# A sparse attention and two expert layers on one core: products with v in two chunks, and copies and sums in another order

## The chip, the core and the metric

The kernel runs on one core of a Trainium2 chip, in one launch. The metric is the device time in microseconds, of which each kernel has several runs; the median counts. Besides the times there is one execution that the hardware profiler recorded. The engines are TensorE (PE in the profile), VectorE (DVE), ScalarE (ACT), GpSimd (POOL) and SyncE (SP), which issues transfers.

## What is computed

An attention over 4 batches of 8 heads, 576 tokens of width 64, in which only scores within tau of a row's greatest are kept; then a layer with eight experts, of which each token uses the one with the greatest gate; then a layer with four experts whose outputs are all summed by given weights. Tokens are 2304, of width 512.

```python
scores = scale * np.matmul(q, k.transpose(0, 1, 3, 2))
thresh = np.max(scores, axis=-1, keepdims=True) - tau
scores = np.where(scores >= thresh, scores, -1000000000.0)
scores = scores - np.max(scores, axis=-1, keepdims=True)
attn = np.exp(scores)
attn = attn / (np.sum(attn, axis=-1, keepdims=True) + 1e-09)
x = np.matmul(attn, v)                      # then 2304 tokens of width 512
...
# first layer: one expert of eight for each token
expert_idx = np.argmax(x @ w_gate, axis=1)  # gate_w: its softmax probability
out[mask] = gate_w[mask, None] * (np.maximum(x[mask] @ w1[e], 0.0) @ w2[e])
...
# second layer: all four experts for each token
out += p[:, e:e + 1] * (np.maximum(x @ w1[e], 0.0) @ w2[e])
```

Sizes: w1 and w2 of the first layer are 8 x 512 x 1024 and 8 x 1024 x 512, of the second 4 x 512 x 1024 and 4 x 1024 x 512, all float32.

## The kernel before

Matmuls run on float32 numbers that are split in two parts: a high part, rounded by a cast ("H"), and a low part, the difference ("low"). A product is then three matmuls (H by H, H by low, low by H). So each operand costs a cast, mostly on ScalarE, and a subtraction, on VectorE or GpSimd.

**Attention** (lines 1040 to 1114) is one loop over 144 steps t: 16 pairs of heads, nine blocks of queries each. A step writes its instructions in a fixed order: the exponential of the block before (`expp`, L751, ScalarE), the scores of the next block (`mm_s`, L733 and L734, TensorE, two banks `s`), the row maximum of its own (`maxx`, L742, VectorE, and `nm`, L745, GpSimd), the mask of two blocks ago (`mask`, L762, VectorE), what waits in the queue `dq` (copies of finished products, L833, VectorE), transpositions of the next pair's q and k (L583), the transpositions of four blocks ago (`transp`, L781 to L799) with their copies `PT` on ScalarE (L785 to L800), one item of the queue `xq`, and items of the products with v. Transpositions and products share four PSUM banks `t`.

The products of a pair are two halves of the queries. Each has five items: `first`, a matmul with the last 64 keys of both heads in one 128 x 128 tile `vl` (L816), and four of two matmuls with 64-column tiles `vt` (L822); a copy `ev` to `outT` follows each half. A matmul is two records in the trace, and two in the rows below that read x2. A pair's items become ready at t = 9p + 13. They go out at steps with t % 3 == 1, as evenly over the chunks left as they divide. In the steady loop these chunks are 4, 3 and 3 items, so that the first half ends within the second chunk. Pair 13 has five chunks. After pair 15 begins (t > 135) another rule spreads them. The queue `xq` holds for each batch the gate's logits, its routing (`route`, L110 to L190: VectorE, ScalarE and GpSimd, with the scatter transfers of rows) and, later, the first expert work; one item goes out in each step.

**First expert layer** (363 to 578 us): 72 weight units, cast and lowered in `split` (L360) as they arrive, by `dosplit`, whose rule gives each unit's low part to VectorE or GpSimd.

**Second layer** (from 589 us): three phases of 768 tokens with 16 steps each (`l1` and `l2`). A step's first product is Strassen-like: seven products of blocks (L1356 to L1358, tile `w`) of the weights' blocks with the tokens' blocks `yc0` to `yc6`, and sums of these on VectorE (`q`, `r`, `c`, L1365; relu on ScalarE, L1370, its low on VectorE, L1371). The first product's result is copied by ScalarE (`p1`, L1375) before VectorE may add to it; then `l1` calls its argument `mid`. The tokens' blocks need four sums (`sums`, L1326: t[1], b12, t[0], t[2]), and each block a cast (L1222) and a low (L1181). `first_blocks` (L1433) writes this for the first step and is its `mid`. Weights come by `prep1(j)` (POOL sums `sx`, ScalarE casts `hl`, GpSimd lows; it casts what it can and returns the cast of `sx` for `mid`) and `prep2(j)` (ScalarE cast `v2hl`, L1212, GpSimd low). The loop at L1445 writes, for step j, `prep1(j + 2)`, `prep2(j + 1)` and the next transfer on SyncE's queue, `l2(j)`, then the `l1` that takes `mid`. Steps 0, 16 and 32 begin a phase.

Of the kernel before, what the change touches and what calls it, by code (L numbers as in the profile page):

```python
# [11 lines left out]
F32 = mybir.dt.float32  # L12
# [3 lines left out]
AF = mybir.ActivationFunctionType  # L16
# [16 lines left out]
def kernel(  # L33
# [99 lines left out]
    def route(t0, nt, pspool, xtile):  # L133
# [35 lines left out]
        for j in range(nt):  # L169
            free_scatter("xs", xs, desti[:, t0 + j : t0 + j + 1], xtile(j))  # L170
        nc.vector.tensor_copy(dest[:, t0 : t0 + nt], desti[:, t0 : t0 + nt])
        yield "scatter"

        ex = small([128, 5, 8], "ex")[:, :nt]
        nc.scalar.activation(ex, d, AF.Exp)
        sg = small([128, 5], "sg")[:, :nt]
# [257 lines left out]
    def dosplit(i, eH=None, eL=None):  # L434
        if i < len(units):
            hls[i] = split(raws.pop(i), eH or "a", eL or ("v" if i % 8 < 3 or i in (3, 4) else "g"), i)

# [18 lines left out]
    def attention(actx):  # L456
# [10 lines left out]

        PG = 3
        NWARM = (36, 3, 3, 3)
# [569 lines left out]
        t = 0  # L1039
        while t < NTT + LT + LP:  # L1040
# [57 lines left out]
            for _ in range(min(len(xq), 1 if t < NTT + LM else 3)):  # L1098
                if xq[0] in frees or not fq and not busy and (xq[0] is not early_start or t >= 9 * last):
                    xq.popleft()()  # L1100
            if pv and (t % PG == 1 or t > 9 * last):
                d = pv[0][2]
                n = max(1, (d + DX - t) // (1 if t > 9 * last else PG))
                n = -(-sum(x[2] == d and x[0].__name__ != "ev" for x in pv) // n)
                while pv and (n or pv[0][0].__name__ == "ev"):
# [210 lines left out]
    with tc.tile_pool(name="m2", bufs=1) as mp, tc.manual_schedule():  # L1316
# [9 lines left out]
        def sums(ph, e):  # L1326
# [3 lines left out]
            for o, a, b_ in ((t[1], b22, b12), (b12, b12, b11), (t[0], b22, b12), (t[2], b21, t[0])):  # L1330
                sub(nc.gpsimd if o is t[2] else e, o, a, b_)
                yield
# [9 lines left out]

        def l1(j, mid, first=False):
            if j >= 3 * NS:
# [39 lines left out]
            prod(Z, 5)  # L1384
            r = add("r", Z, q)
            if not first:
                prod(X, 1, True)
                c11 = relu(0, 0, X)
# [44 lines left out]
        def first_blocks():  # L1433
            for _ in range(3):
                next(ahead)
            for _ in parts2(0, (4, 5, 3)):
                pass
            prep2(0)
            next(ahead)
            for _ in parts2(0, (2,)):  # L1440
                pass

        l1(0, first_blocks, True)
        prep1(1)()
        for j in range(3 * NS):  # L1445
            ph, i = divmod(j, NS)
            if j:
                mid = prep1(j + 2)
            prep2(j + 1)
            fetch2(j + 2 if j == 0 else j + 3)  # L1450
# [48 lines left out]
```

## Time and profile before

| what | value |
|---|---|
| median of 3 runs | 1360.22 us (1359.86 to 1360.77) |
| the profiled execution | 1361.25 us |
| its span in the trace | 1358.8 us |
| TensorE busy | 1323.6 us (97%) |
| GpSimd, VectorE, ScalarE busy | 890.4, 865.9, 653.8 us |
| mean granted clock | 0.993 |

The span runs from the first to the last instruction of the trace; 2.45 us of the profiled execution lie around it. An engine is an in-order queue: an instruction that waits holds what is written behind it. A row of the waits gives the engine and its instruction, what it waited for, and the total, the count and the longest. In a timeline a row is a run of like instructions, with the start of the first, from its start to the last one's end, and what ended the idle time before. TensorE's matmuls overlap, so that the ends of its rows are modelled.

### The profile page before, as it was taken

What the parts mean: (1) busy time and instruction counts of PE and PEld (TensorE: products, weight loads), DVE (VectorE), ACT (ScalarE), POOL (GpSimd) and SP (SyncE); (2) the same over time, 40 slices, a digit from 0 to 9 for tenths busy, and PEclk for the clock granted to TensorE, in tenths of its full rate; (3) what the DMA queues carried; (4) which work ended last, traced back from release to release, by engine and by line L of the source; (5) the groups of instructions that cost most, each with busy time, mean ns of one, the idle gap of its engine ahead of it and who ended that gap; (6) DMA issues with size and microseconds to landing.
All of it is one profiled execution on the core that took longest, in us unless ns stands there. A gap on an engine that the chain in (4) does not pass through costs nothing.

```text
span 1358.8 us, 22300 instructions
## 1 busy us (share of the span) xinstructions
PE 1323.6 (97%) x8120; PEld 1169.4 (86%) x8120; DVE 865.9 (64%) x1705; ACT 653.8 (48%) x1239; POOL 890.4 (66%) x945
## 2 busy tenths in 40 slices
PE   8999999999999999979999999999999999999997
PEld 7777777776899999968999998898999989999986
DVE  8878778777843333545566667666666676655664
ACT  7887786866454455633333334333333343333331
POOL 8876766845385444658666766777677657666642
PEclk8999999999999999989999999999999999999999
DMA  5551111103584556522221112222112222222201
GB/s 153 167 158 57 58 55 62 37 17 110 165 239 148 167 177 203 172 64 78 76 80 62 63 62 67 84 99 78 63 62 76 80 68 80 78 70 78 78 16 47
DMA packets 131696, 127.52 MB, mean 94 GB/s; under 512 B 17920, under 2 KB 110080, under 8 KB 131584
## 3 DMA queue, kind: packets, MB, share of 16 engines
q1 hardware_dynamic: 128128, 116.55, 27.4%
q0 software_dynamic: 3456, 9.51, 1.8%
q8 instruction: 66, 1.08, 0.3%
q14 instruction: 46, 0.38, 0.1%
HBM read 107.61 MB, written 18.42 MB: 93 GB/s over the span
## 4 chain that ended last, share of the span: by engine, by line
PE 68%; issue 3%; POOL 2%; ACT 1%; DVE 1%; POOLq 0%; ACTq 0%; DVEq 0%
PE w L366 14%; PE w L367 14%; PE w L368 14%; PE w L1356 8%; PE w L1358 8%; PE w L1357 8%; PE w L395 1%; PE t L822 0%; DVE g L1371 0%; DVE P L762 0%; POOL out_dram L192 0%; DVE c L1365 0%; POOL hl L360 0%; POOL v2hl L1181 0%; ACT v2hl L1212 0%
## 5 line engine op out<-in xcount | busy, mean ns | idle before, releaser
L1356 PE MATMUL w<-yc,hl 128*128 128x384 f32 x672 | 227.3, 338 | 13.5 <-DVE r L1365 6.5
L1181 POOL TENSOR_TENSOR v2hl<-raw,v2hl 128x1024 fp32r<-128x1024 f32 x48 | 116.0, 2416 | 172.2 <-ACT v2hl L1212 172.2
L1357 PE MATMUL w<-yc,hl 128*128 128x384 f32 x672 | 226.5, 337 | 0.5 <-DVE yc L1181 0.5
L1358 PE MATMUL w<-yc,hl 128*128 128x384 f32 x672 | 226.7, 337 | 0.0
L368 PE MATMUL w<-v2hl,g 128*128 128x512 f32 x576 | 225.3, 391 | 0.0
L366 PE MATMUL w<-v2hl,g 128*128 128x512 f32 x576 | 225.2, 391 | 0.0
L367 PE MATMUL w<-v2hl,g 128*128 128x512 f32 x576 | 224.9, 390 | 0.0
L1420 DVE SCALAR_TENSOR_TENSOR y<-w,big,y 128x512 f32<-128x512 f32 x252 | 179.3, 745 | 51.0 <-PE w L368 50.9
L1370 ACT ACTIVATE g<-c 128x384 fp32r<-128x384 f32 x144 | 75.9, 527 | 191.9 <-DVE c L1365 191.9
L360 POOL TENSOR_TENSOR hl<-raw,hl 128x1024 fp32r<-128x1024 f32 x44 | 107.6, 2446 | 90.6 <-ACT hl L356 55.5
L1371 DVE SCALAR_TENSOR_TENSOR g<-c,g 128x384 fp32r<-128x384 f32 x144 | 111.6, 775 | 62.5 <-ACT g L1370 56.3
L745 POOL TENSOR_SCALAR nm<-nm,sc 128x1 f32<-128x1 f32 x144 | 92.6, 643 | 81.9 <-DVE sb L742 56.0
L1356 PEld LDWEIGHTS w<-yc,hl 128*128 128x128 f32 x672 | 127.0, 189 | 17.3 <-ACT p L1375 7.1
L1212 ACT CAST v2hl<-raw 128x1024 fp32r<-128x1024 f32 x48 | 50.5, 1053 | 188.6 <-PE w L368 188.6
L762 DVE SCALAR_TENSOR_TENSOR P<-sb,nm,E 128x576 f32<-128x576 f32 x144 | 133.5, 928 | 9.1 <-issue 3.0
L1357 PEld LDWEIGHTS w<-yc,hl 128*128 128x128 f32 x672 | 127.1, 189 | 2.6 <-DVE yc L1181 0.8
L368 PEld LDWEIGHTS w<-v2hl,g 128*128 128x128 f32 x576 | 108.3, 188 | 23.6 <-DVE g L1371 0.5
L366 PEld LDWEIGHTS w<-v2hl,g 128*128 128x128 f32 x576 | 108.5, 188 | 21.7 <-ACT g L1370 0.6
L1358 PEld LDWEIGHTS w<-yc,hl 128*128 128x128 f32 x672 | 126.9, 189 | 0.0
L367 PEld LDWEIGHTS w<-v2hl,g 128*128 128x128 f32 x576 | 108.4, 188 | 21.4
L1181 POOL TENSOR_TENSOR hl<-sx,hl 128x1024 fp32r<-128x1024 f32 x48 | 115.6, 2409 | 13.8 <-ACT hl L1196 13.8
L1181 POOL TENSOR_TENSOR hl<-raw,hl 128x512 fp32r<-128x512 f32 x96 | 97.2, 1034 | 41.7 <-ACT hl L1196 41.7
(292 smaller groups left out, 3151.4 us busy)
## 6 DMA issues: line engine op xcount, KB each, us to landing
raw<-in_moe_w_dram SPq DMA_DIRECT2D x168, 512.0 KB
xs<-zrow SPq DMA_DIRECT2D x32, 256.0 KB
xrow<-xs SPq DMA_DIRECT2D x18, 256.0 KB
kt<-in_k_dram SPq DMA_DIRECT2D x16, 256.0 KB
qt<-in_q_dram SPq DMA_DIRECT2D x16, 256.0 KB
vt<-in_v_dram SPq DMA_DIRECT2D x16, 256.0 KB
kt<-in_k_dram SPq DMA_DIRECT2D x16, 32.0 KB
qt<-in_q_dram SPq DMA_DIRECT2D x16, 32.0 KB
```

The source lines that it names most:

```text
L360: e.tensor_tensor(hl[:, 1, :], raw, hl[:, 0, :].bitcast(F32), op=ALU.subtract)
L366: nc.tensor.matmul(o, lhsT=aH, rhs=bH, start=first, stop=False)
L367: nc.tensor.matmul(o, lhsT=aH, rhs=bL, start=False, stop=False)
L368: nc.tensor.matmul(o, lhsT=aL, rhs=bH, start=False, stop=last)
L745: g.tensor_scalar(nm[:, 1:2], nm[:, 0:1], sc[:, 2:3], None, op0=ALU.add)
L762: nc.vector.scalar_tensor_tensor(P, sb, nm[:, 1:2], e, op0=ALU.is_le, op1=ALU.mult, accum_out=a)
L1181: e.tensor_tensor(o, a, b_, op=ALU.subtract)
L1356: nc.tensor.matmul(o, lhsT=aH, rhs=bH, start=first, stop=False, skip_group_check=True)
L1357: nc.tensor.matmul(o, lhsT=aH, rhs=bL, start=False, stop=False, skip_group_check=True)
L1358: nc.tensor.matmul(o, lhsT=aL, rhs=bH, start=False, stop=last, skip_group_check=True)
L1371: return lambda: nc.vector.scalar_tensor_tensor(o[1], src, 0.0, o[0].bitcast(F32), op0=ALU.max, op1=ALU.subtract)
L1420: nc.vector.scalar_tensor_tensor(d, w3(o), s_, d, op0=ALU.mult, op1=ALU.add)
```

## The change

Six edits. `route` writes the gate's exponential before a `yield` and not behind it, one step of the loop sooner. `dosplit` gives the last five units' low parts to VectorE. In the loop the products go out at t % 9 in (0, 5), five items each, with the rule for t > 135 as it was. `sums` gives all four sums to the engine e (VectorE in phase 0, GpSimd in 1 and 2; in the latter it was GpSimd before). `first_blocks` writes the fourth sum behind the first part, the cast of `yc2` ahead of `prep2(0)`, and `last_block`, its low, behind `r`. In the loop, at steps 1, 16 and 32, `prep1` and `prep2` are called in `mid`, thus behind the copy `p1`.

```diff
--- before.py
+++ after.py
@@ -169,10 +169,10 @@
         for j in range(nt):
             free_scatter("xs", xs, desti[:, t0 + j : t0 + j + 1], xtile(j))
         nc.vector.tensor_copy(dest[:, t0 : t0 + nt], desti[:, t0 : t0 + nt])
-        yield "scatter"
-
         ex = small([128, 5, 8], "ex")[:, :nt]
         nc.scalar.activation(ex, d, AF.Exp)
+        yield "scatter"
+
         sg = small([128, 5], "sg")[:, :nt]
         nc.vector.tensor_reduce(sg, ex, axis=AX.X, op=ALU.add)
         yield
@@ -433,7 +433,7 @@
 
     def dosplit(i, eH=None, eL=None):
         if i < len(units):
-            hls[i] = split(raws.pop(i), eH or "a", eL or ("v" if i % 8 < 3 or i in (3, 4) else "g"), i)
+            hls[i] = split(raws.pop(i), eH or "a", eL or ("v" if i % 8 < 3 or i in (3, 4) or i >= len(units) - 5 else "g"), i)
 
     def value(ap, engines, top):
         return nc.values_load(ap, engines=engines, min_val=0, max_val=top, skip_runtime_bounds_check_because=no_need)
@@ -465,7 +465,6 @@
         LE, LM, LT, LP = 1, 2, 4, 1
         DX = 1
 
-        PG = 3
         NWARM = (36, 3, 3, 3)
         ET0 = 140
         g = nc.gpsimd
@@ -1098,10 +1097,9 @@
             for _ in range(min(len(xq), 1 if t < NTT + LM else 3)):
                 if xq[0] in frees or not fq and not busy and (xq[0] is not early_start or t >= 9 * last):
                     xq.popleft()()
-            if pv and (t % PG == 1 or t > 9 * last):
+            if pv and (t % 9 in (0, 5) or t > 9 * last):
                 d = pv[0][2]
-                n = max(1, (d + DX - t) // (1 if t > 9 * last else PG))
-                n = -(-sum(x[2] == d and x[0].__name__ != "ev" for x in pv) // n)
+                n = 5 if t <= 9 * last else -(-sum(x[2] == d and x[0].__name__ != "ev" for x in pv) // max(1, d + DX - t))
                 while pv and (n or pv[0][0].__name__ == "ev"):
                     n -= pv[0][0].__name__ != "ev"
                     f, fin, _ = pv.popleft()
@@ -1328,7 +1326,7 @@
             b11, b12, b21, b22 = blocks(ph)
             t = tb[ph] = [mp.tile([128, 2, HT], F32, tag=f"t{x}", name=f"t{x}") for x in range(3)]
             for o, a, b_ in ((t[1], b22, b12), (b12, b12, b11), (t[0], b22, b12), (t[2], b21, t[0])):
-                sub(nc.gpsimd if o is t[2] else e, o, a, b_)
+                sub(e, o, a, b_)
                 yield
 
         def parts2(ph, ms):
@@ -1340,7 +1338,7 @@
                 in_parts(m, src[m])
                 yield
 
-        def l1(j, mid, first=False):
+        def l1(j, mid, first=None):
             if j >= 3 * NS:
                 return mid()
             h = hs[j] = [mp.tile([128, 2, PT], F32R, tag=f"g{x}", name=f"g{j}_{x}", bufs=2) for x in range(2)]
@@ -1383,6 +1381,8 @@
             q = add("q", Y, p1)
             prod(Z, 5)
             r = add("r", Z, q)
+            if first:
+                first()
             if not first:
                 prod(X, 1, True)
                 c11 = relu(0, 0, X)
@@ -1433,20 +1433,26 @@
         def first_blocks():
             for _ in range(3):
                 next(ahead)
-            for _ in parts2(0, (4, 5, 3)):
-                pass
+            for n, _ in enumerate(parts2(0, (4, 5, 3))):
+                if n == 0:
+                    next(ahead)
+            nc.scalar.copy(yc[2][:, 0], tb[0][2])
             prep2(0)
-            next(ahead)
-            for _ in parts2(0, (2,)):
-                pass
-
-        l1(0, first_blocks, True)
+
+        def last_block():
+            sub(nc.vector, yc[2][:, 1], tb[0][2], yc[2][:, 0].bitcast(F32))
+
+        l1(0, first_blocks, last_block)
         prep1(1)()
         for j in range(3 * NS):
             ph, i = divmod(j, NS)
-            if j:
-                mid = prep1(j + 2)
-            prep2(j + 1)
+
+            if j == 1 or j and i == 0:
+                mid = lambda j=j: (prep1(j + 2)(), prep2(j + 1))
+            else:
+                if j:
+                    mid = prep1(j + 2)
+                prep2(j + 1)
             fetch2(j + 2 if j == 0 else j + 3)
             if j == 0:
                 l2(j)
```

TensorE, in the third pair's steps; `P` are the attention's blocks, `PT` their transposed copies, `t` the banks. Before, at the second of the three chunks of the second pair (`PT_698`), one item of its first half, then `first` and one item of the other:

```order
L781 MATMUL t<-ident,P_1064 128x128 x4
L788 MATMUL t<-ident,P_1028 128x128
L789 MATMUL t<-ident,P_1064 64x128
L822 MATMUL t<-PT_698,vt_457 64x288 x2
L816 MATMUL t<-PT_698,vl_116 128x288
L822 MATMUL t<-PT_698,vt_457 64x288 x2
L733 MATMUL s_1152<-kT_865,qHT_119 128x288
```

After, at the second of its two chunks, two steps later in the loop:

```order
L780 MATMUL t<-ident,P_1131 128x128 x4
L787 MATMUL t<-ident,P_1097 128x128
L788 MATMUL t<-ident,P_1131 64x128
L815 MATMUL t<-PT_698,vl_116 128x288
L821 MATMUL t<-PT_698,vt_457 64x288 x8
L732 MATMUL s_1215<-kT_861,qHT_119 128x288
L733 MATMUL s_1215<-kT_861,qLm_123 128x288
```

Behind the transpositions stand now all five items of one half, with the first half in the first chunk, four steps before; at the place of the rows before, the scores follow the transpositions at once.

VectorE, at the start of the second layer: `t_8570` is the fourth sum, `yc_8549` is `yc2`, `yc_8550` is `yc3`, `yc_8551` is `yc4`, `yc_8552` is `yc5`. Before:

```order
L1181 TENSOR_TENSOR t_8568<-y 128x768
L1181 TENSOR_TENSOR yc_8551<-t_8568,yc_8551 128x768
L1181 TENSOR_TENSOR yc_8552<-t_8569,yc_8552 128x768
L1181 TENSOR_TENSOR yc_8550<-y,yc_8550 128x768
L1181 TENSOR_TENSOR yc_8549<-t_8570,yc_8549 128x768
L1371 SCALAR_TENSOR_TENSOR g_1_8554<-w,g_0_8553 128x384
L1365 TENSOR_TENSOR q<-w,p_8566 128x384
L1365 TENSOR_TENSOR r<-w,q 128x384
L1365 TENSOR_TENSOR c_8622<-w,r 128x384
```

After:

```order
L1179 TENSOR_TENSOR t_8568<-y 128x768
L1179 TENSOR_TENSOR yc_8551<-t_8568,yc_8551 128x768
L1179 TENSOR_TENSOR t_8570<-y,t_8568 128x768
L1179 TENSOR_TENSOR yc_8552<-t_8569,yc_8552 128x768
L1179 TENSOR_TENSOR yc_8550<-y,yc_8550 128x768
L1369 SCALAR_TENSOR_TENSOR g_1_8554<-w,g_0_8553 128x384
L1363 TENSOR_TENSOR q<-w,p_8566 128x384
L1363 TENSOR_TENSOR r<-w,q 128x384
L1179 TENSOR_TENSOR yc_8549<-t_8570,yc_8549 128x768
L1363 TENSOR_TENSOR c_8622<-w,r 128x384
```

The fourth sum, which stood on GpSimd, stands now between the lows of `yc4` and `yc5`, and the low of `yc2` has moved behind `r`.

ScalarE, at step 1 of the second layer; `hl` and `v2hl` are the weights' high parts, `p` the copy, `g` the relus. Before:

```order
L1370 ACTIVATE g_0_8725<-c_8791 128x384
L1196 CAST hl<-raw 128x512
L1196 CAST hl<-raw 128x256
L1212 CAST v2hl<-raw 128x1024
L1375 COPY p_8825<-w 128x384
L1196 CAST hl<-sx 128x1024
L1370 ACTIVATE g_0_8813<-w 128x384
```

After:

```order
L1368 ACTIVATE g_0_8725<-c_8791 128x384
L1373 COPY p_8811<-w 128x384
L1194 CAST hl<-raw 128x512
L1194 CAST hl<-raw 128x256
L1194 CAST hl<-sx 128x1024
L1210 CAST v2hl<-raw 128x1024
L1368 ACTIVATE g_0_8799<-w 128x384
```

The copy `p` stands now ahead of the three casts; the casts of `sx` and `v2hl` have changed places. At steps 16 and 32 it is the same, with other numbers.

## Rows read from the trace of the kernel before

**Rows 1.** The windows view, attention; columns: us, busy by engine, clock, DMA share, GB/s.

```profile
45.30:312.90 267.60, 262.25 (x2026) 201.34 (x2026) 213.24 (x590) 207.25 (x463) 186.36 (x327) 1.00 0.25 78
```

**Rows 2.** What TensorE waited for: total us, times, longest us.

```profile
PE w L1356 <- DVE r L1365: 6.5, 1, 6.5
PE w L1356 <- ACT p L1375: 5.9, 4, 2.0
PE s L733 <- DVE sb L742: 3.7, 11, 0.5
...
PE w L367 <- DVE h L414: 0.4, 1, 0.4
```

**Rows 3.** The windows view, two stretches of the second layer; clock after POOL.

```profile
605.00:610.00 5.00, 5.00 (x16) 3.44 (x15) 3.46 (x7) 3.14 (x6) 1.50 (x2) 0.66 0.00 0
...
630.00:635.00 5.00, 5.00 (x23) 4.78 (x22) 2.93 (x5) 1.05 (x2) 4.84 (x5) 0.77 0.64 201
```

**Rows 4.** TensorE's timeline, one pair: start, us, line, shapes, count.

```profile
66.37 0.62 PE L781 MATMUL t<-ident,P 128*128 128x128 f32 x4
66.92 1.68 PE L822 MATMUL t<-PT,vt 128*64 128x288 f32 x12
...
68.77 0.30 PE L734 MATMUL s<-kT,qLm 128*128 128x288 f32 x1
...
72.24 0.62 PE L781 MATMUL t<-ident,P 128*128 128x128 f32 x4
...
75.12 0.30 PE L734 MATMUL s<-kT,qLm 128*128 128x288 f32 x1
...
79.72 0.27 PE L789 MATMUL t<-ident,P 128*64 128x128 f32 x1
...
81.24 0.71 PE L822 MATMUL t<-PT,vt 128*64 128x288 f32 x4
...
82.11 0.30 PE L734 MATMUL s<-kT,qLm 128*128 128x288 f32 x1
...
82.51 0.60 PE L781 MATMUL t<-ident,P 128*128 128x128 f32 x4
...
83.08 0.29 PE L734 MATMUL s<-kT,qLm 128*128 128x288 f32 x1
```

**Rows 5.** The windows view, one pair's nine steps.

```profile
63.80:82.70 18.90, 18.90 (x147) 14.78 (x146) 15.31 (x38) 15.61 (x35) 13.93 (x23) 1.00 0.28 88
```

**Rows 6.** VectorE's timeline, end of the first layer.

```profile
568.81 2.52 DVE L1181 TENSOR_TENSOR yc<-y,yc 128x768 fp32r<-128x768 f32 x1 [1.24 <-ACT yc L1222]
```

**Rows 7.** VectorE's timeline, start of the second layer.

```profile
592.71 1.83 DVE L1181 TENSOR_TENSOR yc<-t,yc 128x768 fp32r<-128x768 f32 x2 [0.90 <-ACT yc L1222]
...
600.30 1.40 DVE L1181 TENSOR_TENSOR yc<-t,yc 128x768 fp32r<-128x768 f32 x1 [4.89 <-ACT yc L1222]
...
605.74 0.56 DVE L1365 TENSOR_TENSOR c<-w,q 128x384 f32<-128x384 f32 x1 [0.63 <-PE w L1358]
```

**Rows 8.** GpSimd's timeline, the same stretch.

```profile
595.18 2.46 POOL L1181 TENSOR_TENSOR v2hl<-raw,v2hl 128x1024 fp32r<-128x1024 f32 x1 [8.26 <-ACT v2hl L1212]
597.61 1.79 POOL L1181 TENSOR_TENSOR t<-y,t 128x768 f32<-128x768 f32 x1
```

**Rows 9.** ScalarE's timeline, the same stretch.

```profile
594.05 1.05 ACT L1212 CAST v2hl<-raw 128x1024 fp32r<-128x1024 f32 x1
599.44 0.83 ACT L1222 CAST yc<-t 128x768 fp32r<-128x768 f32 x1 [4.33 <-POOL t L1181]
```

**Rows 10.** TensorE's timeline, the same stretch.

```profile
603.44 0.66 PE L1356 MATMUL w<-yc,hl 128*128 128x384 f32 x1 [6.49 <-DVE r L1365]
```

**Rows 11.** ScalarE's timeline, step 1 of the second layer.

```profile
625.64 0.91 ACT L1196 CAST hl<-raw 128x512 fp32r<-128x512 f32 x2
...
627.40 0.47 ACT L1375 COPY p<-w 128x384 f32<-128x384 f32 x1
```

**Rows 12.** TensorE's timeline, step 16.

```profile
863.77 0.44 PE L1356 MATMUL w<-yc,hl 128*128 128x384 f32 x1 [1.60 <-ACT p L1375]
```

## The prediction

> **What bounds the kernel now.** I first read the busy time by stage. In the attention stage (45.3 to 312.9 us) TensorE works 262.25 of 267.60 us [rows 1]; VectorE (213.24) and ScalarE (207.25) have a fifth of the time free. So a saving there must come out of TensorE's own time, not out of another engine's. The view of what TensorE waited for shows what is left beside that: 6.5 us once for VectorE's `r`, 5.9 us in four waits for ScalarE's copy `p`, 0.4 once for `h` in layer 1, and many small ones in attention, the most for `sb`, 3.7 us in eleven waits [rows 2]. The first two kinds are waits of the second MoE layer, whose order the change edits; the first is also followed by a stretch at 0.66 of full clock, and the longest wait for `p` by one at 0.77 [rows 3]. Both rows mix the two levels, 1.2 and 2.4 GHz.
>
> **Products with v: two runs instead of three.** Per head pair the eighteen products (36 records) go out today in three chunks of 4, 3 and 3 items, that is runs of 14, 10 and 12 records; afterwards in two runs of 18. No matmul is removed: what falls is what a run costs beyond its matmuls, when TensorE goes from the transpositions to the products and back to the scores. I price a run as the time from the start of the last transposition before it to the start of the second score matmul (L734) after it. Where no product lies between, that is 82.51 + 0.60 - 0.27 = 82.84 to 83.08, 0.24 us [rows 4] (0.27 is one transposition). With 12 records: 66.72 to 68.77, 2.05. With 14: 72.59 to 75.12, 2.53. With 10, and twice between L822 and L816: 79.72 to 82.11, 2.39 [rows 4]. Less 0.24 each: 1.81 + 2.29 + 2.15 = 6.25 us per pair.
>
> The last four records of the run of 10 (81.24) take 0.71 and the twelve of 66.92 take 1.68, so four more records cost (1.68 - 0.71) / 2 = 0.49 [rows 4]. A run of 18 is the run of 14 plus four: 2.29 + 0.49 = 2.78, two of them 5.56. The saving is 0.69 us per pair, and 13 pairs that go out in three chunks today (0 to 12) give 9.0. Pair 13 goes out in five chunks today and in two afterwards. An extra run costs some 0.34 beyond its records (1.81 - 12 x 0.1225), so about 0.69 + 2 x 0.34 = 1.35. Pairs 14 and 15 keep their rule. Sum: 10.3 us, all on TensorE, so all on the path, if no new wait comes.
>
> **Does a wait come?** The longest stretch without products grows from three steps to five (then four). In the steady pair from 63.8 to 82.7 TensorE works 18.90, ScalarE 15.61 and VectorE 15.31 us in nine steps [rows 5]. Without products a step costs TensorE (18.90 - 6.25) / 9 = 1.41, while ScalarE needs 1.73 and VectorE 1.70. In such a stretch they fall back 0.32 us a step: 0.96 in three steps, 1.6 in five, 1.3 in four, and catch up in a run of 2.78. TensorE writes scores a step ahead, and one of the four transposition banks that an unfinished product holds today is free in the stretch. So I count no wait of its own; the lower bound is the growth, 0.64 + 0.34 = 0.98 per pair, 13 us in all, as a loss. On the other side an unfinished product no longer holds a bank over three steps, which may give back part of the 3.7 us of waits for `sb`. The copies `outT` come at two fixed steps, and the next pair's work behind them starts one step sooner; nothing waits for it today.
>
> **Gate exponentials a step sooner.** The sum `sg` follows the exponential at once on VectorE today, with masks and maxima queued behind it and scores behind those; afterwards a whole step lies between. On ScalarE the exponential moves ahead of one block's copies and delays them by less than one of them. These waits, three in the stage, lie within VectorE's free fifth for the most part. With the banks that come free I take a fifth of the 3.7 us of waits for `sb`, 0.7; the bounds are 0 and all 3.7. Attention: 11.0, between -3 and 14.
>
> **Fourth token sum and low parts on VectorE, end of MoE layer 1.** Five weight lows (units 67 to 71) leave GpSimd. Beside GpSimd's lows VectorE's `yc` lows take 2.52 us today [rows 6], against 1.83 / 2 = 0.92 with GpSimd idle [rows 7]; the rows differ only in that. Five lows of a third more columns (1024 to 768) cost VectorE about 5 x 1.2 = 6.0; three `yc` lows get 1.6 each back, 4.8; and VectorE stands idle 1.24 just ahead of the first [rows 6]. TensorE's wait of 0.4 there for `h` [rows 2] may go: 0.3. The bound on the other side: GpSimd, free sooner, begins the second layer's weight sums and blocks VectorE the same way; then 0.3 is lost.
>
> **The transition.** Today the fourth sum waits on GpSimd behind the `v2hl` low (595.18, 2.46 us) and takes 1.79 until 599.40 [rows 8]; ScalarE stands 4.33 for it, then casts `yc2` in 0.83 [rows 9], the low of `yc2` follows at 600.30 [rows 7], and TensorE's last product of the first step starts at 603.44 after `r` [rows 10]. Its result is read at 605.74 [rows 7].
> Afterwards VectorE does the sum behind the first low of 592.71: 593.6 to 594.55. The lows of `yc5` and `yc3` end at 596.35, ScalarE's cast of `yc2` (0.83) at 595.4 and of `v2hl` (1.05, as at 594.05) at 596.4 [rows 9], the relu at about 596.8. VectorE: the relu's low, `q` and `r` (0.56 each, as the sum at 605.74) end at 598.4, and TensorE's first matmul starts there. The `yc2` low runs 598.4 to 599.3 if alone. GpSimd's `v2hl` low now falls beside it, 596.4 to 598.85. In today's rows the low at 600.30 took 1.40 beside GpSimd [rows 7], and those of layer 1 2.52 [rows 6]; so it ends 599.3 to 600.3. Five more matmuls at 0.32 (half clock, 603.44 to 605.74 today) end at 600.9 to 601.9. Gain 3.9 to 4.8, taken 4.4. From it comes the clock: today the low clock lasts to 608.4, and the busy share will be no better at first, so I charge 1.2 (0 to 3). Net 3.2, between 1.4 and 4.8. What is late next: the weights of the second step, which ScalarE casts behind the relus of the first and GpSimd lowers behind its sums; both move up with the relus, so I count nothing.
> On how `yc2`'s low meets GpSimd, the Trainium skill (SBUF — State Buffer, Who interferes with whom) says that VectorE and GpSimd share one port pair that is an exclusive lock, the loser fully blocked. By that rule the low would stand until 598.85 and end at 599.8, within the span above; the row of 2.52 agrees with it, that of 1.40 blocks less.
>
> **Block products ahead of weight casts.** At step 1 ScalarE's `p` starts at 627.40, behind two `hl` casts (625.64) and the `v2hl` cast [rows 11]. Ahead of them it starts at 625.64, ends at 626.1, and TensorE goes on at 626.15 instead of at 627.92 (`p`'s end, 627.87): 1.77. The stretch at the low level behind it should go: 0.77 over 5 us [rows 3] is 1.15 us of full clock lost there, and it begins before 630, so 1.7 in all (0.5 more by the same rate over some 2 us). At step 16 the wait is 1.60 at 863.77 [rows 12], at step 32 the order is the same, and after these no low clock follows: 2 x 1.6 = 3.2. Sum 6.7; 5.0 if the clock falls anyway. The casts land 0.5 us later, and GpSimd does its `v2hl` low after its `sx` low, one low (some 2.4 us, as at 595.18 [rows 8]) later; SP's next weight load waits for that buffer, but its weights are used a step later. I count nothing.
>
> **Sum.** 11.0 + 0.3 + 3.2 + 6.7 = 21.2 us. The profiled execution took 1361.25, so 1340.05; it lies 1.03 above the median of 1360.22, so 1339.
>
> **Rivals.**
> First, the attention gain is eaten: the growth of the lag (0.98 per pair) is waited out, 13 us against 11 gained. Only 10.2 - 2 remain: 1352; with half of it, 1345. For it: TensorE already waits for `sb` in eleven places [rows 2]. Against it: ScalarE and VectorE have 3.3 us free in each pair of 18.9 [rows 5].
> Second, slower: banks, not the mean load, decide. If TensorE can't run ahead at all and waits for the whole lag, 1.6 + 1.3 per pair and 13.5 pairs make 39 us against 21.2 gained: 1378. It decides from about 0.75 us of wait per chunk. Against it: today 0.96 of lag in three steps gives waits of 3.7 us in the whole stage.
> Third, the transition gains nothing: the low clock stays through the second step and the `yc2` low is blocked. 3.2 is lost: 1342.
> Fourth, more: all 3.7 us of waits for `sb` go (3.0 beyond what I took), and the transition gives its 4.8 with no charge for the clock (1.6 beyond): 1334.
>
> **How the numbers follow.** About 0.2%, 2.7 us, is what a measurement tells from no change. The forecast with the third rival (1336 to 1345): 0.66. First rival (1345 to 1355): 0.16. Fourth (1328 to 1336): 0.10. Slower 0.04, and 0.04 for an attention stage that loses just the rest's gain (within 2.7 us of 1360). Faster 0.92, same 0.04, slower 0.04. The range goes from 1331, most of the fourth, to 1352, the full price of the first.
>
> **What would show it.** Attention: a pair's window falls from 18.9 to about 18.2, waits for `sb`, `PT` or `qLm` stay under 7 us in the stage, and a run of 18 takes about 2.78 + 0.24. Transition: the wait for `r` shrinks from 6.5 to about 2, and the read at 605.74 comes 15 to 16 us sooner (11.3 from the stages ahead, the rest its own). Waits for `p`: from 5.9 to under 1, and full clock in the five microseconds after step 1. I am wrong if the attention stage does not shorten by at least 5, or if waits for ScalarE in it grow to more than that.

## The result and the profile after

The changed kernel takes 1337.88 us (median of 3, 1337.24 to 1338.21) where the kernel before takes 1360.22: a ratio of 0.9835, 95% interval 0.9812 to 0.9857. The forecast was 1339, with a range of 1331 to 1352. Its profiled execution took 1337.24 us, 24.0 less than the one before, where the medians differ by 22.3. The total came out as forecast; the runs below show that two terms of it did not.

What TensorE waited for after the change, the waits that are spoken of here (total us, times, longest):

```profile
PE s L732 <- DVE sb L741: 6.3, 10, 2.5
...
PE w L1354 <- ACT p L1373: 1.1, 2, 0.6
...
PE w L1354 <- DVE r L1363: 1.0, 1, 1.0
```

Against [rows 2]: the wait for `r` went from 6.5 to 1.0 (about 2 was forecast), those for `p` from 5.9 to 1.1 (under 1 was forecast). The waits for `sb`, which were to shrink, grew from 3.7 to 6.3, and one of them is 2.5 us long.

Where the 24 us came, read from the same instruction in both traces (start before less start after). The first `h` is VectorE's first row for layer 1 (L414, `he`), a token sum is the first `t` of the second layer, and `y` are VectorE's rows that take up a step's second product:

| stage | terms forecast | found | read between |
|---|---|---|---|
| attention | 11.0 | 11.7 | the start and the first `h` (348.38, now 336.65) |
| layer 1 | 0.3 | 0.6 | that and the first token sum (588.86, now 576.51) |
| transition | 3.2 | 4.6 | that and the first `y` (608.66, now 591.69) |
| step 1 | 3.5 | 3.1 | first `y` and a `y` of step 1's end (656.29, now 636.19) |
| steps 16 and 32 | 3.2 | 3.6 | that and the last `y` (1348.68, now 1325.01) |

Another execution of the same attention as before (only the copies, below) has its first `h` 0.6 sooner, so attention's 11.7 is known to some 0.6.

**The steady pair** is where the price of a run can be read alone. The windows view of one pair's nine steps after, to be held against 18.90 in [rows 5]:

```profile
65.43:83.67 18.24, 18.19 (x148) 14.93 (x147) 15.18 (x38) 15.35 (x36) 14.00 (x24) 1.00 0.29 93
```

From one exponential to that of nine steps later, the pairs without routing before 100 us take 18.21 to 18.24 each, for 18.89 to 18.93: 0.69, the forecast to its last digit. One run of 18 in TensorE's timeline:

```profile
65.43 0.27 PE L788 MATMUL t<-ident,P 128*64 128x128 f32 x1
65.54 0.65 PE L815 MATMUL t<-PT,vl 128*128 128x288 f32 x2
66.12 2.16 PE L821 MATMUL t<-PT,vt 128*64 128x288 f32 x16
...
68.45 0.29 PE L733 MATMUL s<-kT,qLm 128*128 128x288 f32 x1
```

From the last transposition to the second score matmul it is 68.45 - 65.43 = 3.02, that is 0.24 and the 2.78 of the prediction. (What exactly costs the 0.34 is taken up at the run of ten below.) No wait followed from the longer stretch between runs in these pairs: TensorE is busy 18.19 of 18.24.

**The wait of 2.5 us** is one that the prediction did not look for. Timelines around step 13, first TensorE in the kernel before, then VectorE and TensorE in the changed one:

```profile
33.98 0.65 PE L816 MATMUL t<-PT,vl 128*128 128x288 f32 x2
34.56 1.68 PE L822 MATMUL t<-PT,vt 128*64 128x288 f32 x12
36.69 0.40 PE L733 MATMUL s<-kT,qHT 128*128 128x288 f32 x1 [0.45 <-DVE sb L742]
```

```profile
33.39 0.55 DVE L98 TENSOR_SCALAR w<-i 128x8 f32<-128x8 f32 x1 [1.00 <-POOL i L96]
...
34.42 1.29 DVE L761 SCALAR_TENSOR_TENSOR P<-sb,nm,E 128x576 f32<-128x576 f32 x1
```

```profile
36.45 0.61 PE L732 MATMUL s<-kT,qHT 128*128 128x288 f32 x1 [2.54 <-DVE sb L741]
```

And the windows view of 35 to 40 us, before and after (PEclk is the third number from the right):

```profile
35.00:40.00 5.00, 4.55 (x40) 3.61 (x36) 4.90 (x16) 4.01 (x9) 2.85 (x15) 1.00 0.24 63
```

```profile
35.00:40.00 5.00, 3.55 (x17) 3.12 (x19) 4.90 (x16) 3.75 (x8) 2.85 (x15) 0.66 0.30 83
```

At steps 11 and 12 the kernel writes the first of its set-up: VectorE waits 1.00 for an iota (a row of counted numbers) that stands behind other work on GpSimd, and the mask and the scores behind it come late. VectorE's rows are the same in both kernels (the wait of 1.00 ends at 33.62 in the kernel before). Before, TensorE had pair 0's first run to do there (t % 3 == 1 holds at 13); afterwards this run is at step 14, and TensorE stands 2.54 instead of 0.45 and then works partly at 1.2 GHz.

**The transition.** VectorE, TensorE and GpSimd in the changed kernel, and the clock:

```profile
586.02 1.25 DVE L1179 TENSOR_TENSOR yc<-t,yc 128x768 fp32r<-128x768 f32 x1
...
588.34 0.76 DVE L1369 SCALAR_TENSOR_TENSOR g<-c,g 128x384 fp32r<-128x384 f32 x1 [0.59 <-ACT g L1368]
589.02 0.55 DVE L1363 TENSOR_TENSOR c<-w,q 128x384 f32<-128x384 f32 x1
```

```profile
586.25 0.41 PE L1354 MATMUL w<-yc,hl 128*128 128x384 f32 x1 [0.96 <-DVE r L1363]
587.33 0.44 PE L1355 MATMUL w<-yc,hl 128*128 128x384 f32 x1 [0.67 <-DVE yc L1179]
...
588.31 0.39 PE L366 MATMUL w<-v2hl,g 128*128 128x512 f32 x1
```

```profile
584.09 2.38 POOL L1179 TENSOR_TENSOR v2hl<-raw,v2hl 128x1024 fp32r<-128x1024 f32 x1 [9.66 <-ACT v2hl L1210]
```

```profile
586.00:591.00 5.00, 2.98 (x11) 1.84 (x11) 4.37 (x8) 1.39 (x3) 4.29 (x5) 1.00 0.32 105
```

The read of [rows 7] at 605.74 is at 589.02, 16.7 sooner; this stage began 12.35 sooner (the first sum), so 4.4 are its own, as worked out. Two steps of the working differ and nearly cancel, which is luck: the five matmuls of the first product that follow the one at 587.33 were to take 0.32 each at half clock and took some 0.18 (the next product begins at 588.31), and the read at 589.02 stood on VectorE behind the relu's low (588.34, 0.76), which waited for ScalarE's relu and which the working left out. The wait of 6.49 became two, 0.96 and 0.67, TensorE is busy 2.98 of 5 us, and the clock did not fall: the charge of 1.2 for it did not come. The low of `yc2` met GpSimd's `v2hl` low as expected and took 1.25 for 0.95.

**Step 1.** `p` follows the relu at once, and the stretch behind is at full clock:

```profile
608.45 0.53 ACT L1368 ACTIVATE g<-c 128x384 fp32r<-128x384 f32 x1 [1.30 <-DVE c L1363]
608.88 0.46 ACT L1373 COPY p<-w 128x384 f32<-128x384 f32 x1
```

```profile
609.39 0.44 PE L1354 MATMUL w<-yc,hl 128*128 128x384 f32 x1 [0.50 <-ACT p L1373]
```

```profile
606.00:611.00 5.00, 4.50 (x26) 4.18 (x25) 3.48 (x7) 3.08 (x6) 4.22 (x5) 1.00 0.05 15
611.00:616.00 5.00, 5.00 (x28) 4.57 (x27) 3.48 (x5) 2.42 (x5) 5.00 (x4) 1.00 0.00 2
```

### The profile page after: what moved, and what is told of

The parts are those of the page before. It is cut to its first block, busy times and chain, and to the rows that moved or that the text cites. A ratio compares the mean times of both kernels' runs of the same rounds, so it can differ in the third digit from the quotient of the medians.

```text
span 1335.1 us, 22299 instructions
## 1 busy us (share of the span) xinstructions
PE 1307.3 (98%) x8120; PEld 1168.8 (88%) x8120; DVE 870.1 (65%) x1711; ACT 650.6 (49%) x1239; POOL 880.4 (66%) x939
## 4 chain that ended last, share of the span: by engine, by line
PE 52%; issue 2%; DVE 1%; POOL 1%; ACT 0%; POOLq 0%; DVEq 0%
PE w L368 9%; PE w L366 9%; PE w L367 9%; PE w L1354 8%; PE w L1356 8%; PE w L1355 8%; POOL out_dram L192 0%; POOL v2hl L1179 0%; DVE g L1369 0%; DVE c L1363 0%; DVE t L1179 0%; POOL hl L1179 0%; ACT g L1368 0%; ACT v2hl L1210 0%; POOLq L1500 0%
## 5 line engine op out<-in xcount | busy, mean ns | idle before, releaser
L1369 DVE SCALAR_TENSOR_TENSOR g<-c,g 128x384 fp32r<-128x384 f32 x144 | 114.3, 794 | 61.9 <-ACT g L1368 56.2
L360 POOL TENSOR_TENSOR hl<-raw,hl 128x1024 fp32r<-128x1024 f32 x39 | 94.2, 2417 | 79.5 <-ACT hl L356 55.4
L761 DVE SCALAR_TENSOR_TENSOR P<-sb,nm,E 128x576 f32<-128x576 f32 x144 | 130.2, 905 | 8.9 <-ACT E L750 3.0
```

Source lines behind the costliest of these rows:

```text
L360: e.tensor_tensor(hl[:, 1, :], raw, hl[:, 0, :].bitcast(F32), op=ALU.subtract)
L761: nc.vector.scalar_tensor_tensor(P, sb, nm[:, 1:2], e, op0=ALU.is_le, op1=ALU.mult, accum_out=a)
L1369: return lambda: nc.vector.scalar_tensor_tensor(o[1], src, 0.0, o[0].bitcast(F32), op0=ALU.max, op1=ALU.subtract)
```

## The experiments

Theory: attention gains 0.69 a pair by fewer runs; the rest of its 11.7 is the difference of a new wait at step 13 (about -3.5) and of something else (about +5) that may be the gate's exponential, freed banks, or chance. Medians, each with its ratio to the kernel before run beside it (whose median was 1358.9 to 1360.2):

| kernel | median us | ratio, 95% interval |
|---|---|---|
| changed, again | 1339.19 | 0.9844 (0.9831 to 0.9858) |
| changed, chunk at step 13 | 1337.30 | 0.984 (0.982 to 0.986) |
| changed, exponential late | 1340.86 | 0.9857 (0.9835 to 0.9879) |
| before, only the products | 1353.88 | 0.9956 (0.9939 to 0.9972) |
| changed, three chunks | 1350.69 | 0.994 (0.9919 to 0.9961) |
| changed, set-up sooner | 1335.39 | 0.9819 (0.9806 to 0.9833) |
| changed, scatters apart | 1336.33 | 0.983 (0.9817 to 0.9844) |
| changed, both of these | 1332.58 | 0.9803 (0.979 to 0.9817) |
| both, low parts on GpSimd | 1333.66 | 0.9805 (0.9792 to 0.9819) |
| both, one run of ten | 1345.91 | 0.9896 (0.9881 to 0.9911) |
| both, three chunks | 1353.09 | 0.9951 (0.9937 to 0.9964) |
| before, only the copies | 1355.10 | 0.9964 (0.9952 to 0.9977) |

### Only the products

```diff
-            if pv and (t % PG == 1 or t > 9 * last):
+            if pv and (t % 9 in (0, 5) or t > 9 * last):
...
-                n = max(1, (d + DX - t) // (1 if t > 9 * last else PG))
-                n = -(-sum(x[2] == d and x[0].__name__ != "ev" for x in pv) // n)
+                n = 5 if t <= 9 * last else -(-sum(x[2] == d and x[0].__name__ != "ev" for x in pv) // max(1, d + DX - t))
```

> The kernel before with the products in two chunks and nothing else. By the prediction's price of a run it gains 10.3 us, less the 3.8 lost at step 13, and plus what freed banks give: 1353 to 1354. If the gain in attention beyond this came from banks and not from the exponential, 1349 to 1350.

1353.88, 5.1 less than before, in the middle of the first expectation. By the exponential rows of its trace, 3.6 us are lost between block 12 and block 16 (the wait at step 13), and 10.2 gained from there to block 140: the price of a run (9.6 for pairs 1 to 13) and little else. The 4 us that banks might have given are not there. From block 140 to the first `h` this execution lost 1.5 again: the clock fell (0.64 over 329 to 333) behind a wait of 1.61 for the mask.

### The exponential back

```diff
-        ex = small([128, 5, 8], "ex")[:, :nt]
-        nc.scalar.activation(ex, d, AF.Exp)
         yield "scatter"

+        ex = small([128, 5, 8], "ex")[:, :nt]
+        nc.scalar.activation(ex, d, AF.Exp)
         sg = small([128, 5], "sg")[:, :nt]
```

> The changed kernel with the gate's exponential back behind the yield. The prediction took at most 0.7 us for it together with freed banks, with most of the wait of VectorE covered: 1337.9 to 1338.6. Rival: the pairs with routing gained 5.5 us more than 0.69 each in the trace of the changed kernel, and most of it is VectorE's three waits of 1 to 1.9 us, which TensorE waits out: 1340 to 1342.

1340.86, the rival's size, and in the trace the first `h` stands at 341.76 for 336.65: 5.1 us come back. The medians say less: 3.0 beside the first runs of the changed kernel, 1.7 beside its second (1339.19), and the traced execution (1342.86) is the slowest of four that begin at 1338.55. The traces are firmer on attention: two executions with the exponential late (this one and only the products, the same attention) stand within 0.04 of each other at block 140, two with it sooner (the changed kernel, twice) 0.11 apart, and 5.0 to 5.2 lie between. VectorE and TensorE at the first of the three places:

```profile
142.75 0.19 DVE L177 TENSOR_REDUCE sg<-ex 128x4 f32<-128x32 f32 x1 [2.49 <-ACT ex L175]
```

```profile
143.67 0.40 PE L732 MATMUL s<-kT,qHT 128*128 128x288 f32 x1 [1.44 <-DVE sb L741]
```

In the kernel before VectorE stood 1.83 at this place, and TensorE, with a run of products just ahead (141.23 to 143.26), 0.51:

```profile
146.12 0.40 PE L733 MATMUL s<-kT,qHT 128*128 128x288 f32 x1 [0.51 <-DVE sb L742]
```

At the second, three waits of TensorE from 229 to 234.5 add up to 2.5, and the clock falls behind them (the windows view, 0.69):

```profile
233.00:238.00 5.00, 4.02 (x20) 3.05 (x18) 4.96 (x14) 3.82 (x8) 4.18 (x9) 0.69 0.04 15
```

So the exponential mattered, by waits that VectorE hands on to TensorE.

### Three chunks in the changed kernel

```diff
-            if pv and (t % 9 in (0, 5) or t > 9 * last):
+            if pv and (t % 3 == 1 or t > 9 * last):
...
-                n = 5 if t <= 9 * last else -(-sum(x[2] == d and x[0].__name__ != "ev" for x in pv) // max(1, d + DX - t))
+                n = max(1, (d + DX - t) // (1 if t > 9 * last else 3))
+                n = -(-sum(x[2] == d and x[0].__name__ != "ev" for x in pv) // n)
```

> The changed kernel with the products in chunks as before. By the price of a run it loses 10.3 and gets back 3.8 at step 13: 1344 to 1345. If banks matter, more: up to 1349.

1350.69, more than the price of the runs; the profiled execution, the fastest of the four, took 1347.64, and its first `h` stands at 347.15, 1.2 before the kernel before. That is the most that the exponential is worth with three chunks in a trace: another execution of the kernel before's attention (only the copies, below) stands 0.6 sooner at the first `h` than the one it is held against here, which leaves 0.6. At block 140, ahead of the fall of the clock in one of the traces, the products alone give 6.6, the exponential alone 0.6 to 1.2, both 11.7: the two edits help each other, by some 4 us. The medians agree in direction: two chunks gain 5.1 in the kernel before and 11.5 to 12.8 in the changed one. The rows at step 13 (0.45 for 2.54) and at 143 us (0.51 for 1.44) show how: with a run of products beside it or just ahead of it, most of VectorE's stand is covered. That this holds at each stand of VectorE is argued.

### The chunk at step 13

```diff
-            if pv and (t % 9 in (0, 5) or t > 9 * last):
+            if pv and (t % 9 in (0, 5) and t != 14 or t == 13 or t > 9 * last):
```

> The changed kernel with one step altered: the first chunk of pair 0 goes out at step 13, as in the kernel before, and not at step 14. Theory: at step 13 VectorE stands behind its set-up instructions (it waits 1.00 us for GpSimd's iota in both kernels); in the kernel before a run of products covered this on TensorE, in the changed one TensorE waits 2.54 us for sb at 36.4 us and then works at the low clock from 36.0 to 39.4. With the run back there the wait falls to about 0.5 and the clock stays: 2.1 + 1.7 = 3.8 us, so about 1334 for 1337.9. Rival: the set-up is a bound of its own, the wait comes back a step later, and the time is 1337 to 1338.

The wait at 36.4 and the low clock behind it went, and block 16 came 3.4 us sooner than in the changed kernel. Waits of 0.4, 0.2 and 0.4 in the next steps left 2.3 of it at block 32. Yet the median is 1337.3: in the profiled execution the scores at 229.64 waited 2.48, and there the clock fell, as it had not in the changed kernel's trace:

```profile
229.00:236.00 7.00, 6.36 (x35) 4.24 (x36) 4.87 (x13) 3.73 (x8) 5.98 (x11) 0.76 0.03 10
```

The cause at step 13 stands; its worth of 3.8 was too high in this trace (3.4 to block 16, 2.3 to block 32), and what is won can be lost at the next stall. The median of four does not tell this kernel from the changed one.

### The changed kernel again, set-up sooner, scatters apart, and both

```diff
-                if 11 <= t < 36:
+                if t == 10 or 12 <= t < 36:
                     next(setup, None)
```

```diff
             free_scatter("xs", xs, desti[:, t0 + j : t0 + j + 1], xtile(j))
+            if nt == 5 and j < 4:
+                yield "part"
...
-            for _ in range(ROUTE_STEPS):
+            for _ in range(ROUTE_STEPS + 4 * (b % 2)):
```

> The changed kernel itself, beside the three below, so that they are compared on one chip: 1336 to 1338, with the wait of 2.5 us at 36.4 and the low clock behind it, as in its first trace.

1339.19 (1335.55 to 1339.42). Its trace has the wait of 2.5 at 36.4, and at 232 a second one in place of four small waits. GpSimd, VectorE and TensorE there:

```profile
225.43 1.52 POOL L192 DMA_INDIRECT xs<-X,desti  x1 [0.19 <-issue]
```

```profile
229.84 1.27 DVE L761 SCALAR_TENSOR_TENSOR P<-sb,nm,E 128x576 f32<-128x576 f32 x1 [2.42 <-POOL nm L744]
```

```profile
232.17 0.40 PE L732 MATMUL s<-kT,qHT 128*128 128x288 f32 x1 [2.48 <-DVE sb L741]
```

GpSimd issues five scatters in a row, 0.96 to 1.52 us each with a small memset before it (222.50 to 229.48), and only then `nm`, for which the mask waits, and the next maximum and scores behind it.

> The changed kernel with the first set-up item (GpSimd's iota and select) written at step 10 and not 11; everything else of the set-up, and the chunks, stay. Theory: VectorE's wait of 1.00 us for the iota at 33.4 goes, but its three set-up instructions and the mask slowed to 1.29 stay (2.2 us of the 2.54), so TensorE's wait falls to about 1.5, the clock stays high, and 1.0 + 1.7 = 2.7 us are gained, some of it spent in the small waits behind: 1.5 to 2.7 less than the changed kernel beside it. Rival: the clock falls here whatever the wait, and only 1.0 or less is gained.

1335.39, 3.8 less than the changed kernel beside it. TensorE's wait fell to 0.79, further than worked out, and the clock stayed high:

```profile
35.33 0.40 PE L732 MATMUL s<-kT,qHT 128*128 128x288 f32 x1 [0.79 <-DVE sb L741]
```

In the traces block 140 comes 2.6 us sooner. The wait for the iota was 1.00 of the 1.75 that went. The rest came from VectorE's own rows, which the expectation had left as they were: with other rows of GpSimd beside them, the mask took 0.82 for 1.29 and the second set-up instruction (L99) 0.16 for 0.47; why, no run varied:

```profile
33.77 0.82 DVE L761 SCALAR_TENSOR_TENSOR P<-sb,nm,E 128x576 f32<-128x576 f32 x1
```

> The changed kernel with the five scatter transfers of the second batch's rows on GpSimd written one a step and not all five in one. Theory: they are 1.27 us each and hold nm behind them, VectorE's mask waits for nm, and TensorE loses the 2.0 us at 228 to 232 in four waits; apart, each nm waits for one scatter at most: 1 to 2 us less than the changed kernel beside it. Rival: GpSimd is full in these steps (1.27 + 0.3 + its share of splits in a step of 1.4 us), the nm fall behind all the same, and nothing or a loss of 1 comes.

1336.33, 2.9 less: the wait of 2.48 is gone, one of 0.63 is left at 239.

> Both edits: the sum of the two if the waits are independent, 3 to 4.5 us less than the changed kernel beside it, 1333 to 1334. If a stall that is removed lets the next one grow past the point where the clock falls (as with the chunk at step 13, where the wait at 229.6 became 2.48 and the clock fell), it is the lesser of the two.

1332.58 (1332.50 to 1333.38), 6.6 less than the changed kernel beside it, the sum of the two (3.8 and 2.9) and more than expected. In the traces it is 4.3 at the first `h` (15.95 for 11.62 ahead of the kernel before); the rest of the 6.6 is in medians only. This version beats both kernels. The clock over both places:

```profile
35.00:40.00 5.00, 4.59 (x34) 3.18 (x35) 4.89 (x16) 3.71 (x8) 4.55 (x18) 1.00 0.43 108
228.00:236.00 8.00, 7.65 (x58) 5.65 (x56) 6.21 (x21) 6.47 (x17) 4.26 (x9) 1.00 0.22 85
```

### One run of ten, and three chunks, without the two stalls

```diff
-            if pv and (t % 9 in (0, 5) or t > 9 * last):
+            if pv and (t % 9 == 0 or t > 9 * last):
...
-                n = 5 if t <= 9 * last else
+                n = 10 if t <= 9 * last else
```

> The kernel with both extra edits (set-up sooner, scatters apart; 1332.6) and all ten items of a pair in one run, at t % 9 == 0. By the price of a run: another run less per pair, 2 x 2.78 less (2.29 + 22 x 0.1225) is 0.58, 13 times 7.5 us: 1325. By the lag: nine steps without products let ScalarE and VectorE fall back 9 x 0.32 = 2.9 us where TensorE runs at most about one step of 1.4 ahead; 1.5 or so would be waited out in each pair, 13 x 1.5 = 20 less 7.5: 1345.

(In the diff the ends of the last two lines are left out.) 1345.91, 13.3 more than with two runs, at the lag's 1345; but this is luck, for neither term of that sum held. One run of ten in TensorE's timeline:

```profile
81.31 0.27 PE L790 MATMUL t<-ident,P 128*64 128x128 f32 x1
81.42 0.65 PE L817 MATMUL t<-PT,vl 128*128 128x288 f32 x2
82.00 2.16 PE L823 MATMUL t<-PT,vt 128*64 128x288 f32 x16
84.09 0.75 PE L817 MATMUL t<-PT,vl 128*128 128x288 f32 x2
84.78 2.16 PE L823 MATMUL t<-PT,vt 128*64 128x288 f32 x16
...
87.11 0.29 PE L735 MATMUL s<-kT,qLm 128*128 128x288 f32 x1
```

From the last transposition to the second score matmul it is 5.80, that is 0.24 and 5.56: twice the 2.78 of a run of five. The saving of 0.58 a pair, 7.5 in all, is not there. What fits all the runs is a price not for each run but for each stretch of the 64-column products (`vt`): 0.34 for one by itself (1.81 - 12 x 0.1225 in the prediction). The three chunks have four such stretches, since `vl` parts the middle one; two chunks have two, and 2 x 0.34 is the 0.69 saved; the run of ten has two again, parted by `vl`. No run varied this alone, so it stays a reading of the rows. What TensorE waited for, and the windows view of 18 us of a pair:

```profile
PE s L734 <- DVE sb L743: 8.4, 18, 1.2
PE t L782 <- ACT qHT L641: 2.3, 8, 0.4
```

```profile
65.00:83.00 18.00, 17.66 (x141) 14.54 (x139) 15.03 (x37) 14.33 (x34) 13.38 (x22) 1.00 0.29 93
```

A steady pair takes 18.80 here, for 18.22, so nine steps without products cost 0.58 in such a pair, and not the 1.5 expected; the rest of the 13.3 lies in pairs with routing and in the first ones. TensorE's idle time from block 16 to block 140 is 9.65, for 2.65 with two runs: waits for `sb`, `qHT` and once `qLm`, in most pairs though not in all, though no other engine is busy more than 15.03 of 18 us. This is the prediction's first rival in kind, at nine steps between runs instead of five; in size it is not what the rival's sum gives.

> The kernel with both extra edits (1332.6) and the products in three chunks as before, so that the two chunkings are compared where neither meets the long waits for the set-up and the scatters. By the price of a run alone 10.3 us more: 1342.9. If chunks that end within a half also cost waits that no row of TensorE's idle time shows as such (0.3 us a pair) and those for outT and kT (1.5 in all), 15 to 16 more: 1348.

The edit is that of three chunks above, in the kernel with both extra edits. 1353.09: neither value. Its steady pairs take 18.89, so 0.67 to 0.70 a pair is confirmed. But the scatters apart, which help with two chunks, hurt here: with a run in between, VectorE is late for the copy `outT`, and TensorE finds no free bank. VectorE, TensorE and the clock:

```profile
249.16 1.69 DVE L763 SCALAR_TENSOR_TENSOR P<-sb,nm,E 128x576 f32<-128x576 f32 x1 [2.19 <-POOL nm L746]
...
250.78 0.45 DVE L834 COPY outT<-t 128x288 f32<-128x288 f32 x1
```

```profile
251.28 0.33 PE L789 MATMUL t<-ident,P 128*128 128x128 f32 x1 [1.86 <-DVE outT L834]
```

```profile
252.00:259.00 7.00, 5.59 (x26) 3.75 (x26) 4.94 (x14) 3.26 (x8) 4.92 (x11) 0.52 0.01 0
```

So this run does not isolate the chunking; how much freed banks are worth stays open. The products alone left 0.6 us beyond the price of the runs, and that is net of the waits that they added.

### The low parts of layer 1's end

```diff
-or ("v" if i % 8 < 3 or i in (3, 4) or i >= len(units) - 5 else "g"), i)
+or ("v" if i % 8 < 3 or i in (3, 4) else "g"), i)
```

> The kernel with both extra edits (1332.6) and the low parts of units 67 to 71 back on GpSimd. The prediction took 0.3 us for this edit; between the first and the last h the changed kernel gained 0.9 to 1.2 us. So 1332.9 by the prediction, 1333.6 by the trace: the wait for h near the end of layer 1 comes back, and VectorE's yc lows take 2.5 us for 0.95 to 1.49.

1333.66, 1.1 more; but the kernel before, too, ran 0.9 slower beside it (1360.2 for 1359.3), and the ratios differ by 0.0002, 0.3 us. The medians leave it open. In the traces the way from the first `h` to the first token sum takes 240.35 for 239.73, 0.6. VectorE's low and TensorE's wait are back:

```profile
552.32 2.53 DVE L1181 TENSOR_TENSOR yc<-y,yc 128x768 fp32r<-128x768 f32 x1 [1.25 <-ACT yc L1222]
```

```profile
561.39 0.39 PE L369 MATMUL w<-h,hl 128*128 128x256 f32 x1 [0.38 <-DVE h L416]
```

The last `h` comes 0.9 sooner with the edit, but 0.3 of that is lost again before the token sum; what holds that back these rows do not show. Of ten traces with the edit, eight take 239.6 to 239.9 for this way and none has TensorE's wait for `h`; the other two (exponential late, set-up sooner) take 240.5 and 240.7, with a wait of 0.7 to 0.8 for token rows. The 0.6 is of the size by which executions differ.

### Only the copies

```diff
-            if j:
-                mid = prep1(j + 2)
-            prep2(j + 1)
+            if j == 1 or j and i == 0:
+                mid = lambda j=j: (prep1(j + 2)(), prep2(j + 1))
+            else:
+                if j:
+                    mid = prep1(j + 2)
+                prep2(j + 1)
```

> The kernel before with p1 ahead of the weight casts at steps 1, 16 and 32 and nothing else. By the prediction's terms 6.7 us: 1.77 of the wait at step 1, 1.7 of the low clock behind it, 1.6 twice. Rival: the clock falls at step 1 all the same, or its low stretch lies over waits and costs nothing: 5.0.

The medians differ by 5.1, the rival's figure (3.1 to 6.5 by the interval of the ratio); but this kernel's runs go from 1353.43, the traced one, to 1357.92. In the trace the three steps give 3.4, 1.75 and 1.82, the prediction's terms (1.77 + 1.7, 1.6, 1.6), and the low clock behind step 1 is gone in this execution:

```profile
625.00:630.00 5.00, 4.87 (x29) 4.51 (x28) 3.66 (x6) 4.00 (x8) 4.30 (x4) 1.00 0.02 3
```

The median alone would have chosen the rival. Whether the clock fell behind step 1 in the slower executions no trace shows.

## Why the prediction was right

**Right, by its own steps.** The price of a run: 0.69 a steady pair, 9.6 for the pairs after the first, where the products alone gave 10.2. No wait from the lag at five steps (the first rival). That longer gaps do cost waits is shown at nine steps, though at 0.58 a steady pair and not at the lag's own size, and there the saving of one more run did not come. The transition's chain, 4.4 worked out and 4.4 found, the last link by luck. The copies: 6.7 forecast, 6.7 found in the traces.

**Wrong in two terms that cancel.** That the total came within 1.1 us of the forecast is owed to this, and is luck. First, "all on TensorE, so all on the path, if no new wait comes": the new waits were looked for in the lag of a steady pair alone, and not in what each moved run had covered at its old place. The run at step 13 was the cover of VectorE's stand for the set-up. That wait was in the trace (33.62, 1.00 for the iota, and the scores' wait of 0.45 behind the run). It cost 3.5 to block 16, of which 2.3 to 2.6 could be won back.
Second, "these waits, three in the stage, lie within VectorE's free fifth for the most part" took 0.7 for the exponential and the banks together. It holds with three chunks, where the exponential gave 0.6 to 1.2; with two it gave 5.1 in the traces, of which 1.7 is a fall of the clock, and 1.7 to 3.0 by the medians. A share of free time over the stage says nothing about a wait of 2 us in one step, and the two edits were priced one by one though one takes away the cover of the other. Together: 10.2 - 3.6 for the products and 5.1 for the exponential make 11.7, for 11.0. Two readings under these terms were wrong as well: of the 3.7 us of waits for `sb` only 1.2 lie in the stage from 45.3 to 312.9, the rest mostly ahead of it; and TensorE did wait for `outT` in the kernel before, once, 0.9 us.

**Too small or too large.** Layer 1's end gave 0.6 for 0.3, within what executions differ by. The clock's charge of 1.2 in the transition did not come. Where another execution had the low clock there (set-up sooner, 0.66 over 582 to 587), the stage still took 15.2 from the first token sum to the first `y`, as in the changed kernel (19.8 before), so that it lay over waits; both extra edits had 0.66 there and took 15.2 too.

**On the low of `yc2`.** It began at 586.02 beside GpSimd's `v2hl` low, which ended at 584.09 + 2.38 = 586.47, and took 1.25 for 0.95. The Trainium skill (SBUF — State Buffer, Who interferes with whom) calls the port pair that the two engines share an exclusive lock; if VectorE stood until the other ended, its low would end, by that estimate, at 586.47 + 0.95 = 587.42. The row ends at 587.27, 0.15 sooner, where 0.45 of the two rows overlap. This was within the span that the prediction gave.

## What to carry to other kernels

When work is gathered in fewer and longer runs, ask of each place that a run leaves what it covered there: list the waits of the other engines over one period, not their mean free time, and see which of them had a run beside it. Edits that remove cover and edits that remove waits can't be priced apart; here one was worth at most 1.2 us without the other and 5.1 with it, in the traces. Ask also what a price is a price of: the saving by fewer runs ended at the run of ten, whose second half pays anew. After the change, look for the longest wait left: here an iota written one step sooner and five scatters written one a step gave another 6.6 us by the medians, 4.3 of it in the traces of attention.

## What was not expected of the hardware

The same wait is followed by the low clock in one execution and not in another. TensorE's wait of 1.58 to 1.61 for the mask near the end of attention (it ends at 320 to 330 us) stands in all nine traces with two chunks; behind it the clock fell in the kernel with the set-up sooner and not in the changed kernel beside it:

```profile
322.00:329.00 7.00, 6.78 (x34) 3.09 (x38) 1.08 (x6) 0.75 (x2) 0.00 (x0) 0.76 0.26 77
```

```profile
322.00:329.00 7.00, 5.41 (x38) 2.78 (x36) 3.12 (x3) 1.45 (x4) 2.12 (x2) 1.00 0.22 75
```

It cost 1.65 us there (14.26 gained at block 140, 12.61 at the first `h`). The plainest pair is only the products, where it fell, and the exponential late, where it did not: their attention is the same program. The changed kernel's runs spread over 3.9 us, those of the version without the two long waits over 0.9, and those of scatters apart, which keeps the wait of 2.5 at step 13, over 1.0. So a part of what such a wait costs is the clock behind it; that the spread comes from it too is likely for the wait at 232, and not shown. Which waits are followed by a fall, these runs do not settle: 1.60 at steps 16 and 32 of the kernel before was not; 2.04 at its step 1 and 2.54 at step 13 of the changed one were; and of the wait of 2.48 at 230 to 232 one was (chunk at step 13) and two were not (the changed kernel again, set-up sooner).
